# Dispatch stage of a convolution and soft-MoE kernel: experts' weights loaded ahead of the later x blocks, and the running maximum's product as four column tiles

## The chip, the core and the metric

The kernel runs on one core of one Trainium2 chip. The metric is the device time of one execution in microseconds (us). Engines are named as in the profile: PE is TensorE's matmul, PEld its weight load, DVE VectorE, ACT ScalarE, POOL GpSimd, SP SyncE, which issues nearly all DMAs here.

## The reference

Two stages, all in float32. The first is a long causal convolution with a gate; the second sends all its output tokens through a soft mixture of experts. The dispatch stage, which the change touches, is the part up to `slot_input`.

```python
# x, v: (4, 11456, 128); h_filt: (11456, 128) from a small MLP of pos_emb
y = irfft(rfft(x * v, 2 * S) * rfft(h_filt, 2 * S))[:, :S]
x = (x * y).reshape(45824, 128)                     # tokens
logits = x @ phi                                    # 32 slots = 8 experts x 4
d = softmax(logits, axis=0); slot_input = d.T @ x   # dispatch, over tokens
slot_out[e] = relu(slot_input[e] @ w1[e]) @ w2[e]   # w1: 128x1024, w2: 1024x128
out = softmax(logits, axis=1) @ slot_out            # combine
```

## The kernel before, in words

**Stages.** `conv_part` does the convolution over eight channel groups and writes the gated result by pieces to a DRAM scratch `scr` (`p4_out`, L458). The last pieces are computed while the second stage already starts. `_moe` then works on 358 groups of 128 tokens, in 23 blocks of 16 groups (the last has 6), two blocks to a unit: 12 units. A full block is 128 channels x 2048 tokens, 1 MB.

**One unit of the dispatch stage.** For each unit `m` the loop in `_moe` issues on PE: `turn` of a block (L707: 32 transposes to token-major form, copied out by ACT), `logits(m+1)` of the *next* unit (L773: per block four 32-column products, all of which read the whole block), `turn` of the second block, `dispatch(m-1)` (L865: 32 products of 32 columns), and `running_max(m+1)` (L813), whose result DVE reduces (L814) for the exponentials on ACT (`exps`, L824). The maximum over tokens is thus carried from unit to unit, so one pass is enough. The order on each engine is the program's (`inorder`). So `logits(5)`, which reads blocks 10 and 11, stands on PE between `turn(8)` and `turn(9)`.

**Where blocks live.** `ahead_buf` is five places of 1 MB in the region `ffw`, which later holds the experts' weights: w1 of experts 2i and 2i+1 has the bytes of place i, and w2 of the first two resident experts those of place 4. `xbuf` is five more places (four in `xreg`, one in `E`). Before, blocks 0 to 4 and 10 to 14 go to `ahead_buf`, blocks 5 to 9 and all from 15 on to `xbuf`.

**What sets the order of the loads.** `fetch(i)` is called behind `turn(i)`, which frees block i's place. Before: `fetch(0)` to `fetch(9)` load block i+10; `fetch(10)` to `fetch(13)` the eight w1 (L664); `fetch(14)` the w2 (L667); `fetch(15)` to `fetch(17)` blocks 20 to 22. A block is one to three DMAs, as the pieces of `scr` cut it (L693). SP issues all these in program order, each waiting for its place and for the DMA eight before it on SP, which uses the same one of eight completion semaphores: at most eight are in flight.

Of the kernel before, what the change touches and what calls it, by code (L numbers as in the profile page):

```python
# [17 lines left out]
B, S, D = 4, 11456, 128  # L18
# [27 lines left out]
FF = 1024  # L46
# [585 lines left out]
class Moe:  # L632
# [3 lines left out]
    XB = 5  # L636
# [47 lines left out]

    def load(self, i, d0=0, d1=D):
        q0, n = self.blocks[i]
        t = (self.ahead_buf if i // self.XB in (0, 2) else self.xbuf)[i % self.XB][:, : 128 * n]
        z0, z1 = 128 * q0, 128 * (q0 + n)
        for a, m in self.pieces:
            lo, hi = max(z0, a), min(z1, a + B * m)  # L690
            if lo < hi:
                src = self.scr[D * a : D * (a + B * m)].rearrange("(d t) -> d t", d=D)
                self.tc.nc.sync.dma_start(out=t[d0:d1, lo - z0 : hi - z0], in_=src[d0:d1, lo - a : hi - a])  # L693
        self.xt[i] = t.rearrange("p (q t) -> p q t", t=128)
# [30 lines left out]
def _moe(mo):  # L725
    tc, cp, out, blocks, ctx = mo.tc, mo.cp, mo.out, mo.blocks, mo.ctx
    nc = tc.nc
    NB, XB, OB = mo.NB, mo.XB, mo.OB
# [3 lines left out]
    phis, reps, w1t, w2t = mo.phis, mo.reps, mo.w1t, mo.w2t  # L732

    inorder = tc.keep_in_program_order
# [49 lines left out]
    def maxima(m):  # L784

        mask = pmt[:, 8:12] if m else mo.mask
        if m:
            lts[m] = ms.tile([128, 2 * NB, NSLOT], F32, tag="lt", name=f"lt_{m}", bufs=1)
            rd = ms.tile([128, 2, 4], F32, tag="rd", name=f"rd_{m}")
            rms = [ms.tile([128, 1], F32, tag=f"rm{k}", name=f"rm_{i}") for k, i in enumerate(units[m])]  # L790
        else:
            lts[m] = lt0
            rd = few[3][:, :8].rearrange("p (k a) -> p k a", k=2)
            rms = [few[4][:, k : k + 1] for k in range(2)]
        for k, i in enumerate(units[m]):
            inorder(nc.vector.tensor_reduce(out=rms[k], in_=pls[i].rearrange("p q t -> p (q t)"),
                                            axis=AX.X, op=ALU.max, negate=True))
            inorder(nc.vector.scalar_tensor_tensor(out=rd[:, k], in0=neg[:, m : m + 1].to_broadcast([128, 4]),
                                                   scalar=rms[k], in1=mask, op0=ALU.min, op1=ALU.mult))
            if m and k == 0 and m < last:  # L800
                scores(m, 0)
        return rd[:, : len(units[m])]

    def spread_max(m):
        rd = maxima(m)
        if m < last:
            scores(m, 1)
        return rd

    def running_max(m, rd, pm=None):  # L810
        if pm is None:
            pm = pmt[:, : 4 * len(units[m])]
        inorder(nc.tensor.matmul(pm, lhsT=reps, rhs=rd.rearrange("p k a -> p (k a)"), start=True, stop=True))  # L813
        inorder(nc.vector.tensor_reduce(out=neg[:, m + 1 : m + 2], in_=pm, axis=AX.X, op=ALU.min))  # L814

    def factor(m):
# [124 lines left out]
    def load_w2(e, j):  # L941
        w2t[e] = mo.xbuf[j % XB].rearrange("p (h j d) -> p h j d", h=2, d=128)[:, (e - 3) % 2]
        mo.load_w2(e)

    def fetch(i):
        if i < 2 * XB:
            mo.load(i + 2 * XB)
        elif i < 2 * XB + 4:
            for e in range(2 * (i - 2 * XB), 2 * (i - 2 * XB) + 2):
                mo.load_w1(e)  # L950
        elif i < 3 * XB:
            for e in range(3):
                mo.load_w2(e)
        elif i + XB < NBL:
            mo.load(i + XB)
        else:
            for e in range(3 + 2 * (i + XB - NBL), min(NEXP, 5 + 2 * (i + XB - NBL))):
                load_w2(e, i)
# [9 lines left out]
    rd = maxima(0)  # L968
    for k in range(2):
        scores(0, k)  # L970
    yield
    running_max(0, rd, mo.spot)
    exps(0)
    yield
# [6 lines left out]
    den, fin = (few[5][:, 12 * i :][:, : (1, NU)[i]] for i in range(2))  # L981
    turn(0)
    fetch(0)
    pmt = pp.tile([128, 16], F32, tag="pm", name="pmt")
    inorder(nc.scalar.copy(out=pmt[:, 8:12], in_=mo.mask))
    logits(1)
    rd = spread_max(1)
    turn(1)
    fetch(1)
    pas[0] = pp.tile([128, 128], F32, tag="pa", name="pa_0")  # L990
    warm(4)
    running_max(1, rd)
    factor(0)
    for m in range(1, last - 1):
        u = units[m]
        exps(m)
        if m > LATE:
            invert_unit(m - LATE - 1)
        softmax(m)
        if m > LATE:  # L1000
            scale_unit(m - LATE - 1)
        turn(u[0])
        fetch(u[0])
        turn_weights(m)
        if m > 1:
            collect(m - 2)
        logits(m + 1)
        rd = spread_max(m + 1)
        if m == 2:
            softmax(0)  # L1010
        elif 2 < m <= LATE + 2:
            norm(m - 3)
        turn(u[1])
        fetch(u[1])
        dispatch(m - 1)
        running_max(m + 1, rd)
        factor(m)
    m = last - 1
# [9 lines left out]
    rd = spread_max(last)  # L1028
# [260 lines left out]
```

## Time and profile before

| what | us |
|---|---|
| median of 3 runs | 891.23 (890.74 to 892.21) |
| profiled execution, span from first to last instruction | 888.8 |
| PE busy in that span | 858.3 (97%) |
| dispatch stage, first `turn` to the last `dispatch` | about 737 to 814.5 |

The profiled execution's own device time is not given beside its span; the span is 2.4 us under the median of the runs, which is taken as what lies around it. How to read it: PE is busy nearly throughout, so a microsecond in which PE waits, or that it no longer needs, moves the end. The mean granted clock of TensorE is 0.991.

### The profile page before, as it was taken

To read this page: it belongs to the slowest core of one execution; us is meant where nothing else is said; L and a number is where in the kernel's file an instruction comes from. 1 tells how busy PE (TensorE), PEld (TensorE's weight loads), DVE (VectorE), ACT (ScalarE), POOL (GpSimd) and SP (SyncE) were. 2 spreads that over 40 slices of the span, in tenths; PEclk is the share of its full clock that TensorE was granted. 3 is DMA by queue.
4 is the path that set the end of the run, shared out by engine and by line. 5 is a ranking of instruction groups with operands and counts; after the bars stand their busy time and mean duration, and the time that the engine had idled before them with its cause. 6 is when DMAs were issued, how large, how long until landed. Compare 5 with 4: busy or idle time off the path is not lost. (4 is left out here: it accounts for less than half of the span.)

```text
span 888.8 us, 37282 instructions
## 1 busy us (share of the span) xinstructions
PE 858.3 (97%) x16192; PEld 792.5 (89%) x16192; DVE 714.9 (80%) x1239; ACT 455.9 (51%) x971; POOL 393.3 (44%) x538
## 2 busy tenths in 40 slices
PE   9999999999999999999999999999999999999991
PEld 9998989999999999999999999999999997666540
DVE  5967976898899889988988998899779148886791
ACT  5775558315811751473167128414821637887761
POOL 5003860492088029405910960393079013785750
PEclk9999999999999999999999999999999999999996
DMA  9963685548647755775386476557715979993698
GB/s 329 396 193 117 205 249 148 157 147 269 203 125 210 234 165 141 227 235 167 110 282 201 123 224 207 167 167 238 224 57 166 264 182 374 412 369 121 278 417 364
DMA packets 94386, 197.01 MB, mean 222 GB/s; under 512 B 14330, under 2 KB 55708, under 8 KB 90383
## 3 DMA queue, kind: packets, MB, share of 16 engines
q1 hardware_dynamic: 94046, 194.50, 66.8%
q8 instruction: 127, 2.08, 0.9%
q14 instruction: 37, 0.30, 0.1%
q10 hardware_dynamic: 144, 0.07, 0.0%
q0 software_dynamic: 32, 0.07, 0.0%
HBM read 137.73 MB, written 56.86 MB: 219 GB/s over the span
## 5 line engine op out<-in xcount | busy, mean ns | idle before, releaser
L350 POOL TENSOR_TENSOR T<-m 111x256 f32<-111x256 f32 (+1 forms) x199 | 150.8, 758 | 344.5 <-DVE m L344 344.5
L344 DVE TENSOR_TENSOR m<-p,T 111x1024 f32<-111x1024 f32 (+1 forms) x175 | 200.4, 1206 | 14.4 <-PE p L340 7.0
L360 PE MATMUL p<-tab,T 111*99 111x112 f32 x2048 | 205.4, 260 | 1.5 <-POOL T L351 0.3
L360 PEld LDWEIGHTS p<-tab,T 111*99 111x99 f32 x2048 | 198.8, 170 | 6.5 <-issue 1.6
L340 PE MATMUL p<-T,W 128*64 128x128 f32 (+1 forms) x3168 | 196.7, 276 | 0.4 <-issue 0.3
L420 ACT ACTIVATE vc<-p 128x416 f32<-128x416 f32 x112 | 51.9, 516 | 266.2 <-PE p L411 226.6
L340 PEld LDWEIGHTS p<-T,W 128*64 128x64 f32 (+1 forms) x3168 | 181.8, 127 | 2.7 <-issue 0.9
L411 PE MATMUL p<-tab,E 99*64 99x104 f32 x3584 | 174.1, 252 | 1.1 <-DVE E L373 0.6
L411 PEld LDWEIGHTS p<-tab,E 99*64 99x64 f32 x3584 | 166.4, 136 | 3.1 <-ACT vc L420 0.8
L375 ACT ACTIVATE E<-p 99x448 f32<-99x448 f32 x254 | 132.2, 577 | 63.7 <-PE p L360 57.5
L351 POOL TENSOR_TENSOR T<-m 111x256 f32<-111x256 f32 (+1 forms) x199 | 147.4, 740 | 0.0
L186 ACT ACTIVATE T<-p 128x396 f32<-128x396 f32 x240 | 100.4, 539 | 11.5 <-PE p L174 11.4
L174 PE MATMUL p<-tab1x,x 53*64 53x99 f32 x3648 | 86.7, 246 | 0.2 <-ACT E L224 0.2
L174 PEld LDWEIGHTS p<-tab1x,x 53*64 53x64 f32 x3648 | 79.8, 132 | 4.4 <-ACT E L224 0.4
L436 DVE TENSOR_TENSOR p<-p,vc 128x832 f32<-128x832 f32 x46 | 47.3, 1028 | 10.3 <-ACT vc L420 10.3
L268 DVE TENSOR_TENSOR x<-x,T 128x448 f32<-128x448 f32 x51 | 31.6, 619 | 22.2 <-PE p L174 11.2
L274 DVE TENSOR_TENSOR x<-T 128x224 f32<-128x224 f32 x102 | 39.2, 426 | 1.8
L270 DVE TENSOR_TENSOR T<-x 128x224 f32<-128x224 f32 x102 | 39.2, 425 | 1.7
L224 ACT ACTIVATE E<-fl 111x512 f32<-111x512 f32 (+1 forms) x50 | 26.9, 629 | 21.3 <-PE fl L218 21.3
L444 DVE TENSOR_TENSOR E<-p,E 128x824 f32<-128x824 f32 x36 | 36.6, 1017 | 1.2
L713 ACT ACTIVATE xreg<-pt 128x512 f32<-128x512 f32 (+1 forms) x68 | 35.0, 612 | 0.8 <-PE pt L707 0.7
L344 DVE TENSOR_TENSOR m<-p,E 111x1024 f32<-111x1024 f32 (+1 forms) x25 | 28.7, 1202 | 5.1 <-PE p L340 4.9
(156 smaller groups left out, 972.8 us busy)
## 6 DMA issues: line engine op xcount, KB each, us to landing
x<-in_xf_dram SPq DMA_DIRECT2D x114, 256.0 KB, 4.2
out_dram<-xreg SPq DMA_DIRECT2D x16, 1024.0 KB, 10.5
E<-in_xi_dram SPq DMA_DIRECT2D x37, 412.0 KB, 4.0
T<-in_vf_dram SPq DMA_DIRECT2D x65, 224.0 KB, 5.0
scr<-E SPq DMA_DIRECT2D x67, 206.0 KB, 3.7
T<-hs SPq DMA_DIRECT2D x63, 154.0 KB, 4.5
hs<-E SPq DMA_DIRECT2D x12, 784.0 KB, 4.6
mv<-in_vf_dram SPq DMA_DIRECT2D x42, 224.0 KB, 5.2
```

Of the source, the lines that this page charges most:

```text
L174: inorder(nc.tensor.matmul(ps[h][RP * d : RP * d + RP, i, s, :], lhsT=sd[js, i, s, d, :], rhs=tab1x[js, J * (s + d) : J * (s + d + 1)], st ...
L186: inorder(nc.scalar.activation(dst, src, AF.Copy))
L270: inorder(eng.tensor_tensor(out=vt[:, :, m : m + 2], in0=xr[:, :, 0:2], in1=xr[:, :, 2:4], op=op))
L340: inorder(nc.tensor.matmul(ps[ns, i].rearrange("p b c -> p (b c)"), lhsT=W[:, k0 + i, ns], rhs=Tf[:, :, k0 + i, :], start=True, stop=True, ...
L344: inorder(nc.vector.tensor_mul(m[:, :n].rearrange("p k s e c i -> p k s (e c i)").rearrange("p k s (b c) -> p k s b c", c=CG), ps[:, :n].u ...
L350: inorder(eng.tensor_tensor(out=Ty[:, 0], in0=m[:, :n, 0, 0], in1=m[:, :n, 1, 1], op=ALU.subtract))
L351: inorder(eng.tensor_tensor(out=Ty[:, 1], in0=m[:, :n, 1, 0], in1=m[:, :n, 0, 1], op=ALU.add))
L360: inorder(nc.tensor.matmul(pk[:, i, 2 * s : 2 * s + 2, :].rearrange("p q r -> p (q r)"), lhsT=T[0:N1, s, 2 * k + i, u // 2, :, u % 2], rhs ...
L375: inorder(nc.scalar.activation(dst, src, AF.Copy))
L411: inorder(nc.tensor.matmul(pv[RP * h : RP * h + RP, 2 * k + i, w, :], lhsT=E[:J, r, 2 - 2 * w + s, :], rhs=tab4[:, s, o : o + NJ], start=( ...
L420: inorder(nc.scalar.activation(vc[:, w], pv[:, :, 0, :], AF.Copy, scale=2.0 * w - 1.0))
L436: inorder(nc.vector.tensor_tensor(out=pw, in0=pw[:, 1:2].to_broadcast([128, 2, 4, NJ]), in1=vc, op=ALU.add))
```

## The change

Three edits, all in the second stage.

1. The experts' weights are fetched behind `turn(0)` to `turn(4)` and no longer behind `turn(10)` to `turn(14)`. Blocks 10 to 14 are no longer fetched behind `turn(0)` to `turn(4)`: from block 10 on, each block i+5 is fetched behind `turn(i)` into `xbuf`, so `ahead_buf` holds x once only.
2. Those blocks are loaded in two halves of 1024 tokens, each of which waits only for the readers of its own half of the place.
3. The running maximum's product, one matmul with a 128x128 stationary operand and 8 moving columns, becomes four with a 128x32 stationary operand each, in the four column tiles of the array.

```diff
     def load(self, i, d0=0, d1=D):
         q0, n = self.blocks[i]
-        t = (self.ahead_buf if i // self.XB in (0, 2) else self.xbuf)[i % self.XB][:, : 128 * n]
+        t = (self.xbuf if i // self.XB else self.ahead_buf)[i % self.XB][:, : 128 * n]
         z0, z1 = 128 * q0, 128 * (q0 + n)
-        for a, m in self.pieces:
-            lo, hi = max(z0, a), min(z1, a + B * m)
+        parts = ((z0, z0 + FF), (z0 + FF, z1)) if i >= 2 * self.XB else ((z0, z1),)
+        for a, m, y0, y1 in [(*p, *y) for y in parts for p in self.pieces]:
+            lo, hi = max(y0, a), min(y1, a + B * m)
             if lo < hi:
...
     def running_max(m, rd, pm=None):
...
-        inorder(nc.tensor.matmul(pm, lhsT=reps, rhs=rd.rearrange("p k a -> p (k a)"), start=True, stop=True))
+        for a in range(4):
+            ss = slice(32 * a, 32 * a + 32)
+            inorder(nc.tensor.matmul(pm[ss], lhsT=reps[:, ss], rhs=rd.rearrange("p k a -> p (k a)"),
+                                     start=True, stop=True, tile_position=(0, 32 * a)))
...
     def fetch(i):
-        if i < 2 * XB:
-            mo.load(i + 2 * XB)
-        elif i < 2 * XB + 4:
-            for e in range(2 * (i - 2 * XB), 2 * (i - 2 * XB) + 2):
+        if i < XB - 1:
+            for e in range(2 * i, 2 * i + 2):
                 mo.load_w1(e)
-        elif i < 3 * XB:
+        elif i < XB:
             for e in range(3):
                 mo.load_w2(e)
         elif i + XB < NBL:
```

**The order on SP before**, from the last write of the convolution's result (`scr<-xl`) on; `ffw<-scr`, `xreg<-scr` and `E<-scr` are x blocks, `in_mw_dram` is the experts' weights:

```order
L458 DMA scr<-xl_10646 64x824
L693 DMA ffw<-scr 128x2048
L693 DMA ffw<-scr 128x544
L693 DMA ffw<-scr 128x1504
...
L693 DMA E<-scr 128x640
L693 DMA E<-scr 128x1408
L664 DMA ffw<-in_mw_dram 128x1024 x8
L667 DMA ffw<-in_mw_dram 128x1024 x2
L693 DMA xreg<-scr 128x1476
```

Here blocks 10 to 19 (16 DMAs, 10 MB, from `ffw<-scr 128x2048`, which is block 10, to `E<-scr 128x1408`) stand ahead of ten weight loads of 512 KB, and blocks 20 to 22 behind those.

**The same place on SP with the change:**

```order
L458 DMA scr<-xl_10646 64x824
L664 DMA ffw<-in_mw_dram 128x1024 x8
L667 DMA ffw<-in_mw_dram 128x1024 x2
L694 DMA xreg<-scr 128x1024 x2
L694 DMA xreg<-scr 128x544
L694 DMA xreg<-scr 128x480
L694 DMA xreg<-scr 128x1024 x2
L694 DMA xreg<-scr 128x768
```

The ten weight loads now stand ahead of every block from 10 on, directly behind the same write; block 10 is the first `128x1024 x2`, block 11 the next three DMAs. One w2 load of 512 KB is far earlier on SP in both and doesn't move. Blocks 10 to 22 are 22 DMAs before and 34 now.

**PE before**, from `logits(5)` (`pl`, blocks 10 and 11) over `turn(9)` (`pt`) and `dispatch(3)` (`pa`) to the running maximum (`pmt`) and the first transposes of `turn(10)`:

```order
L773 MATMUL pl_11817<-ffw,aux 32x512 x4
L773 MATMUL pl_11822<-ffw,aux 32x512 x4
L707 MATMUL pt_0_0_11844<-aux,E 128x64
...
L865 MATMUL pa_11886<-xreg,ev_11659 32x128 x16
L865 MATMUL pa_11886<-E,ev_11659 32x128 x16
L813 MATMUL pmt<-rd_11828,aux 128x8
L707 MATMUL pt_0_0_11928<-aux,ffw 128x64
```

**The same place on PE with the change:**

```order
L774 MATMUL pl_11839<-xreg,aux 32x512 x4
L774 MATMUL pl_11844<-xreg,aux 32x512 x4
L708 MATMUL pt_0_0_11866<-aux,E 128x64
...
L869 MATMUL pa_11909<-xreg,ev_11676 32x128 x16
L869 MATMUL pa_11909<-E,ev_11676 32x128 x16
L816 MATMUL pmt<-rd_11850,aux 32x8 x4
L708 MATMUL pt_0_0_11954<-aux,xreg 128x64
```

Nothing changes its place on PE. The products of `logits(5)` read blocks 10 and 11 from `xreg` instead of `ffw`, and the one `128x8` product is now four of `32x8`, of the same column width as the dispatch ahead of them.

## Rows read from the trace of the kernel before

**Rows 1.** Busy time, share of the span and instructions of each engine, whole span.

```profile
PE 858.3 (97%) x16192; PEld 792.5 (89%) x16192; DVE 714.9 (80%) x1239; ACT 455.9 (51%) x971; POOL 393.3 (44%) x538
```

**Rows 2.** Chain of waits, 769 to 786 us: start, length, what.

```profile
769.66 0.32 PE pmt L813 x2
...
770.80 0.95 issue
...
772.34 1.85 PE pl L773 x16
...
777.74 0.42 issue
...
783.83 1.54 issue
```

**Rows 3.** Windows: busy per engine, then granted clock, DMA share, GB/s.

```profile
765.00:772.00 7.00, 5.96 (x143) 4.25 (x136) 5.88 (x11) 6.79 (x16) 5.18 (x7) 1.00 1.02 413
...
779.00:787.00 8.00, 6.46 (x147) 4.40 (x145) 5.24 (x13) 5.96 (x13) 6.88 (x8) 1.00 1.02 407
```

**Rows 4.** DMA issues, 750 to 795 us: KB each, us to landing.

```profile
ffw<-scr SPq DMA_DIRECT2D x1, 528.0 KB, 12.6
xreg<-scr SPq DMA_DIRECT2D x1, 96.0 KB, 12.4
xreg<-scr SPq DMA_DIRECT2D x1, 928.0 KB, 13.1
xreg<-scr SPq DMA_DIRECT2D x1, 1024.0 KB, 5.5
```

**Rows 5.** Timeline of SP's queue, 757 to 795 us: start, length, issues.

```profile
757.94 0.51 SPq L693 DMA_DIRECT2D xreg<-scr  x1
...
759.78 0.32 SPq L693 DMA_DIRECT2D xreg<-scr  x1
...
770.68 12.01 SPq L664 DMA_DIRECT2D ffw<-in_mw_dram  x8
...
794.22 0.32 SPq L693 DMA_DIRECT2D xreg<-scr  x1
```

**Rows 6.** Line L693, 750 to 790 us: ns min/median/max, first and last start.

```profile
L693 SPq DMA_DIRECT2D ffw<-scr x8: 319/396/617, 750.7 to 754.9; - x8
```

**Rows 7.** Timeline of PE, start of the span and 764 to 809 us: start, length, group.

```profile
1.06 3.79 PE L117 MATMUL idle<-E 99*128 99x128 f32 x16 [1.06 <-DVE E L279]
...
764.42 2.22 PE L773 MATMUL pl<-ffw,aux 128*32 128x512 f32 x16
766.57 1.21 PE L707 MATMUL pt<-aux,E 64*128 64x64 f32 x32
...
807.90 1.06 PE L865 MATMUL pa<-xreg,ev 128*32 128x128 f32 x32
808.77 1.06 PE L865 MATMUL pa<-E,ev 128*32 128x128 f32 x32
```

**Rows 8.** Windows at the end and the start, columns as in group 3.

```profile
869.00:873.00 4.00, 0.81 (x8) 0.40 (x6) 1.39 (x4) 1.17 (x4) 0.00 (x0) 1.00 1.01 416
873.00:874.00 1.00, 0.00 (x0) 0.00 (x0) 0.00 (x0) 0.00 (x0) 0.00 (x0) 0.76 1.00 418
...
2.00:5.00 3.00, 3.00 (x16) 3.00 (x15) 0.00 (x0) 2.78 (x10) 2.33 (x3) 1.00 0.96 256
7.00:10.00 3.00, 3.00 (x30) 3.00 (x29) 1.73 (x4) 1.74 (x5) 3.00 (x3) 1.00 1.03 409
```

**Rows 9.** DMA queue of the instructions, whole span: packets, MB, share of 16 engines.

```profile
q8 instruction: 127, 2.08, 0.9%
```

**Rows 10.** Weight loads of the running maximum, a turn and the dispatch.

```profile
762.90 0.30 PEld L813 LDWEIGHTS pmt<-rd,aux 128*128 128x128 f32 x2 [0.20 <-DVE lt L781]
809.76 0.57 PEld L707 LDWEIGHTS pt<-aux,xreg 64*128 64x128 f32 x16 [0.20 <-issue]
...
L865 PEld LDWEIGHTS pa<-E,ev x160: 106/110/110, 754.6 to 809.5; 128*32 128x32 f32 x160
```

## The prediction

> **What bounds the kernel now.** First the busy table: PE works 97% of the span, no other engine over 89% [rows 1], so time is won or lost where PE stands still. Then the chain of waits: in the dispatch stage, once its first units are through, it lies on PE alone. PE stops only three times there, for 0.95, 0.42 and 1.54 us [rows 2], each put down to "issue": it waits for nothing that the profile shows. Together 2.9 us. Third the windows: PE is full, and so are the DMA engines, at 407 to 413 GB/s and a share of 1.0 [rows 3]. No wait of PE for an x block appears; blocks come early enough, but the queue behind them is long: a load issued near 758 takes over 12 us to land [rows 4, 5]. So two things are full at once, and PE is fed from a queue whose *order* the change rewrites.
>
> **Weights ahead of x, the main term.** The weights are meant to load behind the first turns, but SP can't issue them then: they stand behind the convolution's last writes. The DMA that has that place before goes out at 750.7 [rows 6], and so will the first weight. Turns 0 to 4 are over by then, so no weight waits for its place. What arrives when can be read off the trace, since the queue is full and its bytes are served nearly in order. Before, the eight DMAs from 750.7 on are blocks 10 to 14: 5 x 1.05 = 5.24 MB. The last of them (528 KB) is issued at 754.9 and lands 12.6 us later, at 767.5 [rows 4, 6]. The ten weight loads are 10 x 0.524 = 5.24 MB, the same number of bytes, so block 10 now comes in the slot of block 15 and block 11 in that of block 16. Block 15 and the first 96 KB of block 16 have landed at 757.94 + 12.4 = 770.3, the remaining 928 KB at 759.78 + 13.1 = 772.9 [rows 4, 5]. I take block 10 as there at 770.1 and block 11 at 772.9.
>
> PE wants block 10 for `logits(5)` at 764.42 and is done with both at 766.57 [rows 7]. Each block's products take 0.93 us (half of the 1.85 of an undisturbed unit [rows 2]), and all four need the whole block, so the first half's earlier arrival starts nothing. Now they run at 770.1 and 772.9 and end at 773.8: **+7.3 us**. Everything of PE behind them (turn 9, dispatch 3, the maximum) waits too, and DVE and ACT, which live on PE's results, with it. Bounds: the slots move with the transfer rate; 7.34 MB at 413 or at 407 GB/s [rows 3] differ by 0.3 us, which I allow to either side.
>
> **Clock, a cost behind that wait.** PE would stand idle from 764.4 to 770.1, 5.7 us, which it does nowhere between two matmuls before. The nearest row is the end of the kernel: the last matmul ends at 869.8 and the granted clock, 1.00 until 873, averages 0.76 over 873 to 874 on its way to the lower level, 1.2 GHz [rows 8]. The wait is longer than that idle stretch, so I take the clock as fallen when PE resumes. What that costs shows at the start: 16 matmuls in 3 us, later 30 of the same kind [rows 8], half pace, from the first at 1.06 [rows 7] until somewhere between 5 and 7. Four to six slow microseconds from 770.1 end at 774 to 776; up to 772.9 the wait for block 11 covers them, so 1.2 to 3.2 us at half pace cost 0.6 to 1.6. Counted from 772.9 they cost 2 to 3. I take **+1.7**, between; the ends are 0 (no fall) and 3.
>
> **The "issue" stalls, given back.** They come at 770.80, 777.74 and 783.83, and PE runs 6.0 and 5.7 us between them [rows 2]: by the program's order 127 matmuls each time, with as many weight loads. A like count of instructions between stops speaks for packets of instructions; their queue moves 127 packets in 2.08 MB, 16.4 KB each, over the span [rows 9]. I read them as late instruction packets behind a full DMA queue. A PE that is held for 7 us while packets go on arriving has them in stock, so all three vanish: **-2.9**. The other end is 0, if they have another cause or return.
>
> **Running maximum.** Before, it takes 0.32 us for two instructions [rows 2]. Its new neighbours of the same 32-column form are the dispatch's: 32 instructions from 807.90 to 808.77, 27 ns each [rows 7]; eight make 0.22. Seven of the eleven in the loop lie behind `logits(5)` and count, 7 x 0.10 = 0.7; with the last, which stands between transposes, at nothing, **-0.6**. The four ahead end in the wait for block 10. Ends: a single 32-column load of 0.11 us for all four (7 x -0.21 = -1.5), or eight such loads one after another, 0.88 (+3.9) [rows 10]; I take the dispatch's pace, since its four tiles work side by side in the same way.
>
> A rule of the Trainium skill would price this otherwise. The rows show that the weight load of the maximum sits idle for 0.20 us behind the dispatch; a transpose right behind a dispatch, with no maximum between, shows the same 0.20 [rows 10], so I count that idle time as still there, before the transposes. The Trainium skill, "TensorEngine Tiling (Array Packing)", Key Properties, says that a change of tiling mode drains the engine; by that, a maximum in the dispatch's own mode saves one of two drains, and the sum would be 7 x 0.20 = 1.4 us lower.
>
> **Halves and places, at nothing.** Twelve more DMAs on SP, 0.3 to 0.5 us each, lie in its idle time: the eight it issued from 770.68 took 12 us in all, mostly waiting [rows 5]. The weights' 512 KB loads ran at 407 GB/s, the mixture with x's larger ones at 413 [rows 3], so size costs nothing. The later blocks: with an emptier queue a 1 MB block issued at 794.22, block 21, landed 5.5 us later, at 799.7 [rows 4, 5], and nothing waited for it; the new distance of five blocks is the one that block had. Without that slack each odd block would wait.
>
> **Sum.** 7.3 + 1.7 - 2.9 - 0.6 = +5.5 us on the span of 888.8, 894.3. The median of the runs is 2.4 above the span, so 891.23 + 5.5 = **896.7**.
>
> **Rivals.**
> 1. *The clock holds* through the wait: +3.8, **895.0**. For it: two blocks arrive one by one, and the fall after the last matmul is seen once. Against: the wait is longer than that idle stretch.
> 2. *The queue remains the bound.* The instruction packets stay late (+2.9), or odd blocks 15 to 21 miss their products by about 1 us each (+4): **899.6 to 900.7**, say 900.2. For it: the DMA engines stay full until block 17 or so. Against: a block needs 2.6 us of the queue, PE 3.3 us or more, so the queue empties.
> 3. *Nothing waits, faster.* Block 10 lands by 764.4, block 11 by 765.4, the late packets are gone with the weights out of the stretch from 770 to 787, and all eleven maxima save 0.1: -2.9 - 1.1 = -4.0, **887.2**. It decides at the rate: 5.24 + 2.1 MB from about 754.6 (767.5 less 5.24 MB at 407) to 765.4 would need 680 GB/s, against 413. Or x would have to overtake weights in the queue, where the landings [rows 4] come in order.
> 4. *A drain fewer*, by the mechanism weighed above: +4.1, **895.3**. For it: the 0.20 idle ahead of each maximum. Against: the same 0.20 ahead of transposes.
> 5. *The wait is much shorter*, as if the weights had been issued as early as the change means them to be: within 0.2%. Against: SP's order.
>
> **Chances.** Forecast 0.51, clock holds 0.22, queue remains 0.12, a drain fewer 0.05, nothing waits 0.06, short wait 0.04. A measurement of this kernel can tell about 0.2%, 1.8 us, from no change. Faster by more: 0.06 (rival 3). Within: 0.04 (rival 5). Slower: 0.90. The range reaches from the clock that holds with a drain fewer (893.6) to the returned stalls (900.2), with 0.2 for the rate on either side: 893.4 to 900.4. What lies outside is rivals 3 and 5 and half of rival 2.
>
> **What would show it.** The chain of waits has one new idle stretch of PE ahead of the first products of `logits(5)`, about 5.7 us, released by the DMA of block 10, and a shorter one of 1 to 2 us for block 11; SP issues the weights from 750.7 and block 10 near 759; the window at 770 to 776 has a granted clock under 1.00; the three "issue" stalls are gone; the maximum takes 0.2 instead of 0.32 us. The prediction is wrong if PE runs through `logits(5)` at 764 to 766, if the waits repeat in later units, or if the stalls remain.

## The result, and the profile after

The changed kernel takes **899.17 us** (897.54 to 903.05, 5 runs), the kernel before, run beside it, 891.23 us (5 runs): ratio **1.0087**, 95% interval 1.007 to 1.0104, slower by 7.9 us. The forecast was 896.7, range 893.4 to 900.4. The profiled execution, 899.17 us itself, has a span of 897.4 us, 8.6 more than before. The busy rows stay within 1.4 us of what they were [rows 1], PE's to the tenth, with 72 more matmuls, so the longer span shows as idle time of PE.

The busy row on the profile's page of the changed kernel:

```profile
PE 858.3 (96%) x16264; PEld 792.2 (88%) x16264; DVE 716.3 (80%) x1239; ACT 454.7 (51%) x971; POOL 392.7 (44%) x538
```

SP's queue (timeline: start, length, issues) shows the new order as forecast: weights from 750.94, in the place that blocks 10 to 14 had [rows 6], then the blocks.

```profile
750.94 5.40 SPq L664 DMA_DIRECT2D ffw<-in_mw_dram  x8
756.43 1.87 SPq L667 DMA_DIRECT2D ffw<-in_mw_dram  x2
759.27 13.37 SPq L694 DMA_DIRECT2D xreg<-scr  x10
```

PE's timeline (start, length, group; in brackets the idle time ahead and its releaser), around `logits(5)` and in the units behind it. In [rows 7] the same `logits(5)` runs at 764.42 without a wait and turn 9 starts at 766.57.

```profile
763.73 0.90 PE L708 MATMUL pt<-aux,xreg 64*128 64x64 f32 x22 [0.99 <-issue]
772.40 1.94 PE L774 MATMUL pl<-xreg,aux 128*32 128x512 f32 x8 [7.77 <-DMA xreg<-scr]
775.12 1.94 PE L774 MATMUL pl<-xreg,aux 128*32 128x512 f32 x8 [0.78 <-DVE rm L797]
776.98 1.97 PE L708 MATMUL pt<-aux,E 64*128 64x64 f32 x32
778.88 1.40 PE L869 MATMUL pa<-xreg,ev 128*32 128x128 f32 x32
780.10 1.05 PE L869 MATMUL pa<-E,ev 128*32 128x128 f32 x32
780.97 0.21 PE L816 MATMUL pmt<-rd,aux 128*32 128x8 f32 x8
781.12 1.21 PE L708 MATMUL pt<-aux,xreg 64*128 64x64 f32 x32
...
789.10 1.07 PE L774 MATMUL pl<-E,aux 128*32 128x512 f32 x8 [0.32 <-ACT et L828]
...
807.62 0.25 PE L816 MATMUL pmt<-rd,aux 128*32 128x8 f32 x8 [0.41 <-DVE rd L799]
808.70 0.90 PE L708 MATMUL pt<-aux,xreg 64*128 64x64 f32 x22 [0.38 <-issue]
...
818.69 0.52 PE L708 MATMUL pt<-aux,xreg 64*128 64x64 f32 x9 [0.25 <-issue]
```

PE stands for 7.77 us until block 10 is there. The second wait is put down to DVE, but in the runs below in which PE is quick there, the same gap is released by a DMA: it is block 11, 2.7 us behind block 10. The chain of waits (start, length, what) runs through the loads, where before it ran through PE [rows 2]:

```profile
752.44 8.04 DMA ffw<-in_mw_dram
...
760.54 11.72 DMA xreg<-scr
...
772.40 1.97 PE pl L774 x8
...
775.12 1.94 PE pl L774 x8
```

The windows (busy time per engine, granted clock, DMA share, GB/s) show the clock. Before it was 1.00 all through [rows 3].

```profile
765.00:766.00 1.00, 0.00 (x0) 0.00 (x0) 0.59 (x2) 1.00 (x3) 0.81 (x1) 0.96 1.01 406
766.00:768.00 2.00, 0.00 (x0) 0.00 (x0) 0.00 (x0) 1.11 (x2) 0.74 (x1) 0.50 1.02 410
...
775.00:779.00 4.00, 3.88 (x44) 2.13 (x48) 2.46 (x6) 0.87 (x2) 0.00 (x0) 0.50 0.52 204
779.00:780.00 1.00, 1.00 (x31) 0.95 (x34) 0.00 (x0) 1.00 (x3) 0.00 (x0) 0.71 0.89 119
780.00:781.00 1.00, 1.00 (x48) 1.00 (x42) 0.00 (x0) 0.37 (x2) 0.00 (x0) 1.00 0.90 363
```

The last matmul ends at 764.63; at 766 the clock is at its lower level, 1.2 GHz, and it stays there until PE has worked again for some microseconds behind block 11. Each piece at half pace can be read off the rows: 1.94 for the eight matmul records of one block's `logits` (0.93 at full pace), 1.97 for turn 9 (1.21 in [rows 7]).

**The account.** Turn 10 starts at 781.12, before at 769.91: +11.2. At full pace `logits(5)` would end at 775.12 + 0.93 = 776.05, against 766.57: waits +9.5. Half pace behind block 11: products 0.93, turn 0.76, dispatch 0.3, together +2.0. The maximum gives back 0.27 (shown below). From turn 10 to the end of the dispatch (823.16, before 814.47) the kernel wins 2.5 again: five maxima of 0.27 each, 1.35, and 1.5 because 3.07 us of stops (2.91 "issue" [rows 2], 0.16 ACT) became 1.57 (the last four bracketed rows above, with one of 0.21 for ACT), less 0.3 that no row names. What is left is +8.7.

The maximum itself, in the timeline of PE's weight loads of the changed kernel, between a dispatch and a turn:

```profile
793.14 0.90 PEld L869 LDWEIGHTS pa<-E,ev 128*32 128x32 f32 x32
794.02 0.24 PEld L816 LDWEIGHTS pmt<-rd,aux 128*32 128x32 f32 x8
794.28 1.07 PEld L708 LDWEIGHTS pt<-aux,E 64*128 64x128 f32 x32
...
817.99 0.32 PEld L708 LDWEIGHTS pt<-aux,xreg 64*128 64x128 f32 x7 [0.20 <-issue]
```

The 0.20 us of idle time ahead of the maximum [rows 10] is gone, and none has come ahead of the turn. Where a turn stands right behind the dispatch, at 817.99, the 0.20 is there in the changed kernel too. From the start of a dispatch to the start of the turn behind it PE takes 1.93 to 1.98 us in the units without a stop or half pace; before it took 2.20 to 2.30.

### The profile page after: what moved, and what is told of

Read it like the earlier page. It is cut to its first block, busy times and chain, and to the rows that moved or that the text cites. A ratio compares the mean times of both kernels' runs of the same rounds, so it can differ in the third digit from the quotient of the medians.

```text
span 897.4 us, 37454 instructions
## 1 busy us (share of the span) xinstructions
PE 858.3 (96%) x16264; PEld 792.2 (88%) x16264; DVE 716.3 (80%) x1239; ACT 454.7 (51%) x971; POOL 392.7 (44%) x538
## 5 line engine op out<-in xcount | busy, mean ns | idle before, releaser
L411 PE MATMUL p<-tab,E 99*64 99x104 f32 x3584 | 176.0, 252 | 1.2 <-DVE E L373 0.6
L411 PEld LDWEIGHTS p<-tab,E 99*64 99x64 f32 x3584 | 168.2, 136 | 3.4 <-ACT vc L420 0.8
L186 ACT ACTIVATE T<-p 128x396 f32<-128x396 f32 x240 | 100.2, 537 | 11.2 <-PE p L174 11.1
```

Of the source, the lines that this page charges most:

```text
L186: inorder(nc.scalar.activation(dst, src, AF.Copy))
L411: inorder(nc.tensor.matmul(pv[RP * h : RP * h + RP, 2 * k + i, w, :], lhsT=E[:J, r, 2 - 2 * w + s, :], rhs=tab4[:, s, o : o + NJ], start=( ...
```

## The experiments

The theory after the result: the order of the loads makes the whole cost (a wait, and the clock that falls in it); the stops come from instruction packets behind a full DMA queue; the four tiles are worth what PE's instruction supply lets through.

**1. The loads without the tiles** (`loads_alone`): the change, with the maximum as one product again.

```diff
-        for a in range(4):
-            ss = slice(32 * a, 32 * a + 32)
...
+        inorder(nc.tensor.matmul(pm, lhsT=reps, rhs=rd.rearrange("p k a -> p (k a)"), start=True, stop=True))
```

> The changed kernel with the running maximum as one product. Theory: the wait for blocks 10 and 11 and the lower clock come from the loads alone, and behind the wait the packets are in stock, so four tiles do save their 0.16 us there, seven times: 1.1 us slower than the changed kernel, 899.5 to 900.5. Rival (the four tiles save nothing anywhere): 899, as the changed kernel.

Measured: 899.28 us, ratio 1.0074 (1.0054 to 1.0094), within the noise the changed kernel's own time: the rival's case, and not the 1.1 us more that the theory expected. PE's timeline has the same two waits:

```profile
773.36 1.94 PE L774 MATMUL pl<-xreg,aux 128*32 128x512 f32 x8 [7.85 <-DMA xreg<-scr]
776.04 1.93 PE L774 MATMUL pl<-xreg,aux 128*32 128x512 f32 x8 [0.74 <-DVE rm L797]
```

So the loads alone cost what the change costs. Behind the waits this kernel has 0.42 us of stops, where the changed one has 1.57: most of the 1.6 us that six tiled maxima save there is lost again in stops.

**2. The tiles without the loads** (`rm4_alone`): before, with the maximum as four tiles.

```diff
-        inorder(nc.tensor.matmul(pm, lhsT=reps, rhs=rd.rearrange("p k a -> p (k a)"), start=True, stop=True))
+        for a in range(4):
...
```

> The kernel before, with nothing but the running maximum as four column tiles. The profile of the changed kernel shows the maximum at 0.15 to 0.16 us where it was 0.32. Theory: PE bounds the units behind the first ones, so 0.16 us times the seven to eleven maxima that lie on PE's path come back, 1.1 to 1.7 us: 889.5 to 890.1. Rival: PE is fed by the instruction queue in the stretch with the 'issue' stalls and there only waits longer, so a part is lost again: 890.3 to 891.0, with the three stalls together longer than 2.9 us. Second rival: four times as many small products cost as much as they save: no change.

Measured: 892.16 us, ratio 1.0002 (0.999 to 1.0014): nothing; the interval leaves room for a gain of 0.9 us, under the 1.1 to 1.7 expected. Ten units are 0.27 us shorter, but PE's stops in the timeline grow from 2.91 to 4.93 us:

```profile
764.84 0.90 PE L707 MATMUL pt<-aux,xreg 64*128 64x64 f32 x22 [0.97 <-issue]
771.45 0.31 PE L868 MATMUL pa<-E,ev 128*32 128x128 f32 x4 [0.96 <-issue]
777.64 1.08 PE L868 MATMUL pa<-xreg,ev 128*32 128x128 f32 x32 [0.22 <-issue]
790.22 0.78 PE L707 MATMUL pt<-aux,xreg 64*128 64x64 f32 x19 [0.79 <-issue]
795.92 0.62 PE L773 MATMUL pl<-xreg,aux 128*32 128x512 f32 x2 [0.76 <-issue]
812.51 0.40 PE L707 MATMUL pt<-aux,xreg 64*128 64x64 f32 x6 [1.23 <-issue]
```

Each tiled maximum is 12 instructions more. A PE that runs quicker through more instructions comes to the end of its supply sooner.

**3. Fewer bytes in the queue** (`no_weights`): before, without its ten weight loads. Those weights are never loaded; the arithmetic is the same in number and shape.

```diff
-            for e in range(2 * (i - 2 * XB), 2 * (i - 2 * XB) + 2):
-                mo.load_w1(e)
+            pass
...
-            for e in range(3):
-                mo.load_w2(e)
+            mo.load_w2(2)
```

> The kernel before without its ten weight loads behind turns 10 to 14 (so the experts' products read what x left there). Theory: the three 'issue' stalls are instruction packets that come late because the DMA queue is full; without the weights the queue is empty from about 781 on, so the stalls at 771 and 778 stay and the one at 784 (1.54 us) goes: 889.3 to 890. Rival (the packets come at a fixed pace, whatever the queue does): all three stay, 891. Second rival (it is the place in the program): all three stay.

Measured: 890.22 us, ratio 0.9978 (0.9964 to 0.9992). PE's timeline keeps the first two stops, as long as before, and loses the third, 1.54 us:

```profile
772.33 0.58 PE L707 MATMUL pt<-aux,ffw 64*128 64x64 f32 x11 [0.95 <-issue]
778.73 1.15 PE L707 MATMUL pt<-aux,ffw 64*128 64x64 f32 x30 [0.42 <-issue]
```

and its windows say why: the first two fall while the DMA engines are still full with x (share 0.96 from 771 to 772.4, and the first row here).

```profile
772.00:779.00 7.00, 6.25 (x135) 4.32 (x137) 5.25 (x12) 5.75 (x13) 4.93 (x6) 1.00 0.95 382
779.00:786.00 7.00, 7.00 (x175) 5.21 (x170) 6.06 (x13) 6.76 (x16) 5.93 (x5) 1.00 0.06 22
```

In the kernel before, each stop ends some 2.5 us after a packet of the instruction queue has moved: of the half microseconds from 769.0, 775.5 and 782.5 each moves one (the row is from 775.5), and PE resumes at 771.75, 778.16 and 785.37. In the change it is the same: packets start to move at 761.2, 806.3 and 816.4, and PE resumes at 763.73, 808.70 and 818.69. The stops are late instruction packets.

```profile
q8 instruction: 1, 0.02, 12.8%
```

**4. Weights later** (`weights_spread`): the change, with the ten weights one by one behind turns 6, 8 and so on to 19, and blocks 10 and 11 ahead of them.

```diff
-        if i < XB - 1:
-            for e in range(2 * i, 2 * i + 2):
-                mo.load_w1(e)
...
+        if i in (6, 8, 10, 12, 14, 16):
+            inorder(mo.load_w1(i // 2 - 3))
+        if i == 18:
+            for e in (6, 7):
+                inorder(mo.load_w1(e))
+        if i == 19:
+            for e in (0, 1):
+                inorder(mo.load_w2(e))
```

> The changed kernel (x from block 10 on in five places, by halves, maximum as four tiles), but the ten weight loads stand behind x: six of them one by one behind turns 6, 8, ... 16, four behind turns 18 and 19. Theory (the wait is the bytes that stand ahead of blocks 10 and 11 in a full queue): no wait of PE for block 10, clock 1.00 throughout, and since the queue is never full for long the 'issue' stalls shrink: 887 to 890. Rival (five places are too near, whatever stands ahead): odd blocks come late unit after unit, 893 or more, with DMA waits ahead of the logits' products in several units.

Measured: 892.31 us, ratio 1.0012 (0.9999 to 1.0026). Neither wait is left, and some 7 us of the change's cost are gone: that part of the theory stands. The further gain that was expected is not there: the stops stay at 3.4 us, and the weights now keep the DMA engines full until 810 (share 0.93 to 1.04). One stop does more harm than its length (timeline and windows of this kernel):

```profile
798.97 0.90 PE L708 MATMUL pt<-aux,xreg 64*128 64x64 f32 x22 [1.53 <-issue]
799.80 3.59 PE L774 MATMUL pl<-xreg,aux 128*32 128x512 f32 x16
```

```profile
799.00:800.00 1.00, 1.00 (x26) 0.89 (x30) 1.00 (x2) 0.59 (x2) 1.00 (x1) 0.96 1.04 402
800.00:802.00 2.00, 2.00 (x12) 0.43 (x8) 0.56 (x3) 1.48 (x4) 2.00 (x3) 0.50 0.92 348
```

The sixteen matmuls of `logits` take 3.59 us at the lower clock, 1.92 undisturbed.

**5. Spread weights, whole blocks, one product** (`spread_plain`): as 4, without halves and without tiles.

> x from block 10 on in five places and the weights spread behind turns 6 to 19, but whole blocks and the running maximum as one product again. Theory: 24 PE instructions fewer in a unit than with four tiles, so PE needs its instruction packets less often, and fewer, larger x pieces: the 'issue' stalls sum to less than the 3.4 us of the spread version and less than the 2.9 of the kernel before: 889.5 to 890.8. Rival (the queue is as full as before, so the stalls are too): 891 to 892.

Measured: 892.43 us, ratio 1.0 (0.9986 to 1.0013). Stops of 1.32, 0.79 and 1.09 us, with the DMA engines as full as before (share 0.87 to 1.03 up to 812; the last stop falls behind that): the expected gain did not come. With and without tiles the time is the same (4 against 5), as between 1 and the change.

**6. Four weights ahead** (`four_ahead`): four loads ahead of block 10, the others behind turns 8 to 16.

```diff
-        if i < XB - 1:
+        if i < 2:
             for e in range(2 * i, 2 * i + 2):
                 mo.load_w1(e)
```

> The changed kernel with four weight loads ahead of block 10 instead of ten; four more behind turns 8 to 14, two behind turn 16. Theory: 3.15 MB less ahead of block 10 at 0.405 MB per us is 7.8 us, so it lands near 764.5, as PE comes for it: wait under 1 us, for block 11 about 1.5 us, no fall of the clock; 889 to 892. Rival (the wait is set by the time at which turns 5 and 6 free the places, not by what stands ahead): 898 to 900, as with ten.

Measured: 893.64 us, ratio 1.0025 (1.0012 to 1.0039). No wait for x, clock 1.00; the forecast of 889 to 892 missed, with stops of 4.2 us.

**7. Seven weights ahead** (`seven_ahead`), the dose between:

```diff
-            for e in range(2 * i, 2 * i + 2):
+            for e in range(2 * i, min(7, 2 * i + 2)):
...
+        if i == 12:
+            inorder(mo.load_w1(7))
```

> The changed kernel with seven weight loads ahead of block 10 in place of ten: the eighth goes behind turn 12, the other three behind turn 16. Three loads less are 1.57 MB, 3.9 us of the queue at 405 KB per us. Theory (the wait is the bytes ahead, the clock falls in the wait whatever its length beyond 1 to 2 us): PE waits 3.9 us for block 10 instead of 7.8, the second wait stays near 0.8, the granted clock is again 0.5 for some us, and the time is 3.9 less than that of the changed kernel: 895.3. Rival one (a shorter wait leaves the clock at 1.00): 2 to 3 us less again, 892.5 to 893.3. Rival two (a shorter wait puts fewer instruction packets in stock, so that the late packets come back by 1 to 2 us): 896.3 to 897.3.

Measured: 896.98 us, ratio 1.006 (1.0041 to 1.0079): rival two's time, though not by its cause. PE's timeline and windows:

```profile
764.13 0.90 PE L708 MATMUL pt<-aux,xreg 64*128 64x64 f32 x22 [0.98 <-issue]
767.08 1.78 PE L774 MATMUL pl<-xreg,aux 128*32 128x512 f32 x8 [2.04 <-DMA xreg<-scr]
769.71 1.94 PE L774 MATMUL pl<-xreg,aux 128*32 128x512 f32 x8 [0.86 <-DVE rm L797]
771.58 1.97 PE L708 MATMUL pt<-aux,E 64*128 64x64 f32 x32
...
810.62 0.49 PE L869 MATMUL pa<-xreg,ev 128*32 128x128 f32 x9 [1.86 <-issue]
```

```profile
811.00:812.00 1.00, 1.00 (x36) 0.98 (x27) 0.73 (x4) 0.50 (x1) 0.00 (x0) 0.83 0.43 147
812.00:815.00 3.00, 3.00 (x58) 2.47 (x58) 2.66 (x5) 3.00 (x9) 1.71 (x1) 0.50 0.59 201
```

Block 10 comes 5.3 us sooner than in the change, more than the expected 3.9. The clock falls with a wait of 2.04 us too: the second block's products and the turn take what they took in the change, so its price is the same for both waits, and does not go by their length. Turn 10 starts 5.4 us sooner than in the change (775.69), but the dispatch ends only 2.5 sooner (820.70). Of the 3.0 us between, 1.2 are longer stops, one of 1.86 at 808.8 with the DMA engines at 0.98, and 1.5 are a second fall of the clock right behind it: from the maximum at 810.86 to the turn at 815.99 PE takes 5.13 us, in the change 3.65 (814.34 to 817.99). Rival two expected late packets from a smaller stock after a shorter wait; this stop comes some 40 us after it, while the weights that were moved behind turns 12 and 16 load.

**8. The wait filled** (`wait_filled16`): the change, with 16 matmuls into an unused tile ahead of `logits(5)`, so that PE works while it waits.

```diff
+        if m == 4:
+            idle = pp.tile([128, 128], F32, tag="pa", name="idle_pa")
+            for _ in range(16):
+                inorder(nc.tensor.matmul(idle, lhsT=reps, rhs=ident, start=True, stop=True))
```

> As with 32 fillers, but 16 of them, some 4.5 us, which end before block 10 lands (32 lasted 9.0 us and began 1.2 us late, so they outlasted the wait). Theory: only some 2 us of idle time are left ahead of the landing, the clock stays at 1.00, the two logits take 0.93 us each again and the 3.0 us of the lower clock come back: 896 (895.5 to 897). Rival (the wait alone carries the cost, the slow products are hidden behind block 11): 898.5 to 899.5.

Measured: 896.24 us, ratio 1.0053 (1.0034 to 1.0071). PE's timeline and windows:

```profile
765.49 5.43 PE L1012 MATMUL idle_pa<-aux 128*128 128x128 f32 x32 [1.14 <-DVE xreg L874]
771.40 1.07 PE L774 MATMUL pl<-xreg,aux 128*32 128x512 f32 x8 [0.48 <-DMA xreg<-scr]
773.98 1.06 PE L774 MATMUL pl<-xreg,aux 128*32 128x512 f32 x8 [1.51 <-DMA xreg<-scr]
774.97 1.21 PE L708 MATMUL pt<-aux,E 64*128 64x64 f32 x32
```

```profile
766.00:768.00 2.00, 2.00 (x12) 2.00 (x11) 0.00 (x0) 0.84 (x1) 1.02 (x1) 0.50 1.01 401
768.00:770.00 2.00, 2.00 (x16) 2.00 (x16) 0.00 (x0) 0.00 (x0) 1.73 (x4) 0.78 1.05 401
770.00:772.00 2.00, 1.52 (x17) 0.91 (x15) 0.00 (x0) 0.00 (x0) 0.24 (x1) 1.00 1.02 400
```

The clock had fallen in the 1.14 us ahead of the filling and came back during it, so PE meets both blocks at the full clock: turn 9 takes 1.21 again. Turn 10 is 3.1 us sooner than in the change: 2.0 by the clock, 1.1 because block 11 landed that much earlier in this run, which is chance for the most part: the last part of its load came 0.9 us behind the others, in the change 1.7 (see the first point of the next section). The gap ahead of the second products is released by the DMA, as said above.

**9. The same with 32 matmuls** (`wait_filled`):

> The changed kernel, with 32 matmuls of 128x128 without use on PE between turn 8 and the logits of blocks 10 and 11, some 8 us of work at full pace, so that PE is busy while it waits for block 10. Theory: the lower clock behind the wait costs 2.0 us in the two logits, 0.8 in turn 9 and 0.2 in dispatch 3, 3.0 in all; with the clock kept at 1.00 the time falls to 896 (895.5 to 897). Rival (what is slow behind the wait is the data, not the clock): 899 as before, with the two logits still 1.9 us each; or slower, if the filling lasts longer than the wait.

Measured: 899.06 us, ratio 1.0082 (1.0051 to 1.0113), a miss by its design: the filling began 1.15 us late, lasted 9.0 us, outlived the wait, and put its own work in the place of what it saved.

**10. Without the halves** (`whole_blocks`):

```diff
-        parts = ((z0, z0 + FF), (z0 + FF, z1)) if i >= 2 * self.XB else ((z0, z1),)
+        parts = ((z0, z1),)
```

> The changed kernel without the halves: blocks from 10 on are loaded whole, in the five places. Theory (all four products of logits(5) need a whole block, and the queue moves halves as fast as whole blocks): 899.2 as the changed kernel, within 0.9, with a wait of 7.8 us for block 10. Rival (the halves help, as the smaller loads come sooner): 1 to 2 us slower, 900 to 901. Other rival (a dozen more DMA issues on SP cost something): 0.5 to 1 us faster.

Measured: 900.1 us (897.57 to 901.0), ratio 1.0078 (1.0051 to 1.0105), at the edge of the bound given for no effect and within the rival's 900 to 901; by the ratio, which takes the kernel beside it, no slower than the change (1.0087). Block 11 follows block 10 by 2.55 us, as with halves (2.72). The wait for block 10 is 4.47 us and not the expected 7.8, since a stop of 1.36 us at 760.0, with half pace behind it, had already held PE back.

## Why the prediction held, point by point

- **Weights ahead of x: the mechanism as forecast, the size too small.** +7.3 was forecast, +9.5 came. The step that failed is the landing in "block 10 now comes in the slot of block 15": 770.1 and 772.9 were taken, the first products started at 772.4 and 775.1. A load lands in sixteen parts, each with an event of its own in the trace, and PE starts behind the last. Of block 10's second half, issued at 760.54, fifteen parts had landed at 770.56 and the sixteenth at 772.26. Of the DMA at 757.94, which closes that slot before [rows 5], fifteen had landed at 770.09 and the sixteenth at 770.30. From the first issue (750.94, before 750.67) to the fifteenth part it is 19.6 us against 19.4, so the bytes did come in that slot. The forecast missed the 0.27 us by which the weights go out later, and one part that runs 1.7 us behind the others in place of 0.2; for block 11 it does so too (773.20, then 774.91). How far it lags differs from run to run: 1.6 us in run 1, 1.0 in run 10, 0.9 in run 8, 0.6 in run 7. In the change the lag begins with a weight load that landed at 761.61 and 763.30, and an instruction packet moves just ahead, at 761.2; whether that packet holds the part up is not shown.
- **Clock: right.** +1.7 forecast, +2.0 by the rows, and run 8 gives the 2.0 back. Rival 1, that the clock holds, is refuted. The reading of the end of the kernel as the nearest row was too mild, though: there the fall shows 3 to 4 us after the last matmul, here after less than 1.4.
- **"issue" stalls: the cause right (run 3), the saving half.** -2.9 was forecast for stops that vanish. 0.63 us of them came back later in the stage, and 0.94 us of waits for ACT and DVE took some of their place: -1.5. The reason given, packets that "go on arriving" while PE is held, is not what the trace shows: PE stands from 764.6 to 772.4, and after the packet at 761.2 the next one moves at 776.5, when the DMA share is down to 0.35 (776 to 779). Up to 799 packets then come every 5.1 to 6.3 us and PE has no "issue" stop; the one at 806.3 comes 7.1 us behind the one before, and PE stands again.
- **Running maximum: -0.6 forecast, -1.6 measured, and rival 4's outcome, one idle stretch fewer, was the right one.** By [rows 10] the idle 0.20 us was counted as still there, ahead of the turn. But that row is of a turn right behind a dispatch, and there the 0.20 stays (817.99). Between the dispatch, the maximum and the turn the changed kernel has it nowhere; a maximum in the dispatch's own form saves 0.27 us and not 0.10. The Trainium skill, "TensorEngine Tiling (Array Packing)", Key Properties, says that a change of tiling mode drains the engine; the trace agrees where another form follows the dispatch (0.20 us), and shows no such idle time between the maximum and the turn, which are of different forms too. Rival 4's time, 895.3, was wrong all the same, because of the first point. In the kernel's time the saving shows nowhere: runs 1 and 2 and the pair 4 and 5 each show none beyond the noise, 0.1 to 0.3%. That it would show with the packets in time, no run tests.
- **Halves and places: 0, as forecast** (run 10). No later block is waited for, which refutes one half of rival 2; its other half, packets that stay late, came true by about half.

The sum was 7.3 + 1.7 - 2.9 - 0.6 = +5.5; by the same terms it is 9.5 + 2.0 - 1.5 - 1.6 + 0.3 = +8.7. The two smaller terms missed by 1.4 and 1.0 us in opposite directions, which is luck. The median grew by 7.9 and not by 8.6, since the profiled execution lies 1.8 us over its span, where the forecast took 2.4. By the number alone rival 2 (900.2) was nearer than the forecast; the waits and the clock in the rows tell them apart.

No version beats the kernel before: with the loads in another order and the tiles, 892.3 to 893.6 were the best.

## What to carry to other kernels

When loads are moved within a full queue, the bytes put ahead of a block delay it, whatever turn the code names for the issue: read from SP's timeline when the issue can really go out, and from the landing events when the last part of a load is there. A wait on PE costs its length and, where the clock falls in it, what PE then does at half pace, here 2 us behind a wait of 2.0 and of 7.8 us alike. And in a stage in which PE gets its instructions late, faster matmuls gave no time here: first look at what shares the DMA engines with the instructions.

## What the runs showed of the hardware

- The granted clock fell in the change 1.4 us behind the last matmul at the latest. In other runs it fell in, or within 1.1 us behind, shorter stops: 2.04 and 1.86 us (run 7), 1.53 (run 4), 1.36 (run 10) and 1.14 (run 8). It stayed at 1.00 through a stop of 1.54 us in the kernel before (at 783.8), of 1.32 in run 5 and of 1.26 in run 6. What makes the difference was not tried.
- In the kernel before, with the DMA engines full, an instruction packet moves every 6.0 to 7.2 us from 757 to 795. PE needs one for some 254 instructions (32384 matmuls and weight loads to 127 packets of queue q8 [rows 1, 9], in the change 32528 to 128), which it runs in 5.7 to 6.0 us [rows 2]. Its stops come from that, and what four tiles save was lost again in longer ones (run 2).
- A load was there for PE with the last of its sixteen parts, and in the loads that landed near 770 that part lagged the other fifteen by 0.2 us in the kernel before and by 1.7 in the change, both with the DMA engines full.
- The maximum's eight matmuls (32 stationary and 8 moving columns each) take 0.15 us from their start to the turn's, 19 ns each; those of the dispatch, with 128 moving columns, 27 ns [rows 7].
